# Three zero fills that run on fifteen DMA engines, without engine 2, in a decode step's forward and backward pass

## The chip, the cores and the metric

One core of a Trainium2 chip runs the whole program. The metric is the device time of one execution in microseconds (us); lower is better. Each kernel is run several times beside the kernel before, on the same chip, and all the runs that were compared here were in the fast state except one single run, of unknown state, which is marked. The kernel before takes 631.31 us (median of three runs, 631.11 to 631.31).

## The reference, cut to what matters

The reference is a transformer decode step of one token (attention over the last 4096 rows of a cache of 65,536, a gated MLP and modulated layer norms) together with its gradients. Two of its eleven outputs are the gradients of the two caches. Only the last 4096 of their 65,536 rows can be non-zero:

```python
W = min(4096, max(256, Sk // 4))                       # Sk = 65536, so W = 4096
k = jnp.repeat(k_cache[:, :, Sk - W:, :], rep, axis=1)
v = jnp.repeat(v_cache[:, :, Sk - W:, :], rep, axis=1)
...
_out, _vjp = jax.vjp(_f, A_x, A_k_cache, A_v_cache, ...)
return (_out0, *[jnp.asarray(_g) for _g in _grads])    # 2 x 4 heads x 61440 rows of zeros
```

So the kernel has to write 2 x 4 x 61,440 x 128 bf16 zeros, 120 MB (of 1024 KB each), besides loading the weights and storing their gradients.

## The kernel before

The zeros are written in 120 fills of 1 MB, issued by GpSimd wherever the schedule has room for them. Lists of counts (Z_FFN, Z_DWO and others) say how many follow each step.

```python
ZW = 4096
zeros = vt([P, ZW // 2], "zeros", FP8)            # 128 x 2 KB of zeros in SBUF
...
for og in (out_2, out_3):
    for g in range(G):
        region = og[0, g, 0:SKW, :].rearrange("r d -> (r d)").rearrange("(p x) -> p x", p=P)
        for i in range(region.shape[1] // ZW):
            zregions.append(region[:, i * ZW:(i + 1) * ZW])
zleft = list(zregions)
...
def zero(n, after=None):
    for _ in range(n):
        if len(zleft) <= keep[0]:
            return
        # per row: 2 KB of fp8 zeros in, a region of 8 KB seen as fp32 out
        ins = nc.gpsimd.dma_start(out=zleft.pop(0).bitcast(FP32), in_=zeros[:, :])
        if after is not None:
            dep(ins, after)
```

A fill has 128 rows of 8 KB. I take it as spread evenly over the 16 DMA engines of the page, 64 KB for each: at a sixteenth of the 429 GB/s that the program moves from 606 to 612 us, 64 KB takes 2.44 us, and successive fills near the end land 2.45 us apart. Most gradients are stored by GpSimd's DMAs as well; the rows of eight that Sync stores (`col_to_row_out`, in the trace eight packets of 256 bytes each) come up once below. The last DMA lands at 625.98 us, 3.5 us before the span ends.

## Time and profile before

| | before |
|---|---|
| median time | 631.31 us |
| span of the profiled run | 629.5 us |
| bytes moved by DMA | 256.42 MB, mean 407 GB/s |
| last landing, first of its 16 increments | 619.09 us |
| last landing, fifteenth increment | 620.75 us |
| last landing, sixteenth increment | 625.98 us |

From the page of the kernel before, the busy times of the compute engines, and the row of the DMA issues that belongs to the zero fills (count, size of one, median time from issue to landing):

```profile
PE 185.2 (29%) x3324; PEld 162.1 (26%) x3324; DVE 325.8 (52%) x728; ACT 212.8 (34%) x333; POOL 141.0 (22%) x224
...
out_dram<-zeros POOLq DMA_DIRECT2D x120, 1024.0 KB, 17.5
```

No compute engine is near its limit (52% at most), and a fill lands 17.5 us after its issue although one engine's share of it takes 2.45 us: about seven are in the queue (17.5 / 2.45). The remaining views of the kernel before are shown in the prediction.

Two ways of reading are used all through this text. A **landing** is the set of sixteen semaphore increments of one DMA; they stand in the trace with their times. I read them as one from each of the 16 DMA engines: between the fifteenth of the last landing (620.75 us) and its sixteenth (625.98) the program moves 20 to 26 GB/s, about a sixteenth of the 429 before. No record says which engine sent which. A **late** engine shows as a sixteenth increment far behind the fifteenth.

### The profile page before, as it was taken

To read this page: it belongs to the slowest core of one execution; us is meant where nothing else is said; L and a number is where in the kernel's file an instruction comes from. 1 tells how busy PE (TensorE), PEld (TensorE's weight loads), DVE (VectorE), ACT (ScalarE), POOL (GpSimd) and SP (SyncE) were. 2 spreads that over 40 slices of the span, in tenths; PEclk is the share of its full clock that TensorE was granted. 3 is DMA by queue.
4 is the path that set the end of the run, shared out by engine and by line. 5 is a ranking of instruction groups with operands and counts; after the bars stand their busy time and mean duration, and the time that the engine had idled before them with its cause. 6 is when DMAs were issued, how large, how long until landed. Compare 5 with 4: busy or idle time off the path is not lost.

```text
span 629.5 us, 8417 instructions
## 1 busy us (share of the span) xinstructions
PE 185.2 (29%) x3324; PEld 162.1 (26%) x3324; DVE 325.8 (52%) x728; ACT 212.8 (34%) x333; POOL 141.0 (22%) x224
## 2 busy tenths in 40 slices
PE   3877175632031211111111113304910022226100
PEld 3877155622021211111111112201700012225000
DVE  2442045204986784647565456999730089920400
ACT  2651156200035352424343233984700022225300
POOL 1001011103314232325312342222111013212320
PEclk9875588755555555555555555555755555555555
DMA  9999999999999999999999999999999999999994
GB/s 350 425 419 421 420 421 419 425 423 427 421 380 397 402 400 406 405 402 407 410 401 406 385 411 411 420 421 424 423 424 426 425 419 428 427 427 423 422 427 160
DMA packets 42183, 256.42 MB, mean 407 GB/s; under 512 B 4768, under 2 KB 4768, under 8 KB 17568
## 3 DMA queue, kind: packets, MB, share of 16 engines
q0 software_dynamic: 31104, 192.95, 80.2%
q1 hardware_dynamic: 10992, 62.93, 29.0%
q8 instruction: 26, 0.43, 0.3%
q14 instruction: 13, 0.11, 0.0%
q10 hardware_dynamic: 48, 0.01, 0.0%
HBM read 70.26 MB, written 185.60 MB: 406 GB/s over the span
## 4 chain that ended last, share of the span: by engine, by line
DMA 66%; DVE 13%; PE 6%; ACT 5%; issue 4%; POOL 3%; ACTq 0%; POOLq 0%; SPq 0%; DVEq 0%
DMA out_dram<-arena 35%; DMA arena<-in_B_w_gate_dram 8%; DMA arena<-in_A_wq_dram 7%; DVE arena L177 7%; DMA arena<-in_A_v_cache_dram 6%; DMA out_dram<-zeros 4%; DMA arena<-in_A_wo_dram 4%; ACT arena L791 1%; ACT arena L208 1%; DVE arena L181 1%; DVE fold_ps L181 1%; POOL out_dram L623 1%; PE tp_kv L407 1%; DMA rows<-in_c_dram 1%; POOL arena L506 1%
## 5 line engine op out<-in xcount | busy, mean ns | idle before, releaser
L142 POOL DMA_DIRECT2D out_dram<-zeros x120 | 65.5, 550 | 213.6 <-DMA out_dram<-zeros 58.5
L208 ACT ACTIVATE arena<-dug_b,h 128x512 bf16<-128x512 bf16 x112 | 71.4, 713 | 13.2 <-DVE dh2acc L177 12.1
L177 DVE CUSTOM_DVE_ANT_0 arena<-arena,dug_b 128x512 bf16<-128x512 bf16 x112 | 69.6, 684 | 0.4
L177 DVE CUSTOM_DVE_ANT_0 arena<-arena 128x1024 bf16<-128x1024 bf16 (+1 forms) x16 | 45.1, 2818 | 46.6 <-DMA arena<-in_w_mod_dram 39.2
L579 PE MATMUL gu_ps<-h_bf,arena 128*128 128x1 bf16 x448 | 16.0, 166 | 129.9 <-issue 97.8
L787 PEld LDWEIGHTS <-arena 8*128 8x128 bf16 x256 | 24.7, 127 | 105.8 <-issue 102.7
L579 PEld LDWEIGHTS <-arena 128*128 128x128 bf16 x448 | 14.1, 105 | 131.9 <-issue 98.3
L177 DVE CUSTOM_DVE_ANT_0 junk<-arena,b1k 128x1024 fp8e4<-128x1024 bf16 x28 | 34.2, 1223 | 15.1 <-DMA arena<-in_B_w_down_dram 14.6
L177 DVE CUSTOM_DVE_ANT_0 arena<-arena,b1k 128x1024 bf16<-128x1024 bf16 x32 | 37.2, 1219 | 0.0
L505 POOL DMA_DIRECT2D arena<-in_B_w_up_dram x14 | 12.7, 910 | 105.2 <-DMA out_dram<-arena 93.3
L791 ACT CAST arena<-ps_kv 128x512 bf16<-128x512 f32 x32 | 16.1, 696 | 59.7 <-DMA out_dram<-arena 59.7
L581 ACT ACTIVATE sg<-gu_ps 128x2 f32<-128x2 f32 x14 | 2.4, 171 | 94.8 <-PE gu_ps L579 94.8
L787 PE MATMUL ps_kv<-DO_hd,arena 8*128 8x128 bf16 x128 | 15.2, 277 | 60.5 <-ACT arena L791 59.7
L208 ACT ACTIVATE arena<-b1k,o_sh 128x1024 bf16<-128x1024 bf16 x24 | 27.2, 1152 | 11.0 <-DVE do_sh L177 11.0
L793 ACT ACTIVATE arena<-ps_kv 128x512 bf16<-128x512 f32 x32 | 16.1, 627 | 38.8 <-DMA out_dram<-arena 38.8
L169 DVE COPY arena<-tp_kv 128x1024 bf16<-128x1024 bf16 x19 | 13.0, 690 | 30.4 <-PE tp_kv L407 30.3
L407 PE MATMUL tp_kv<-ident_bf,arena 128*128 128x128 bf16 x256 | 21.8, 251 | 23.3 <-DMA arena<-in_A_k_cache_dram 13.7
L787 PE MATMUL ps_kv<-Q_hd,arena 8*128 8x128 bf16 x128 | 16.1, 296 | 38.9 <-ACT arena L793 38.9
L407 PEld LDWEIGHTS <-arena 128*128 128x128 bf16 x256 | 19.0, 114 | 26.1 <-DMA arena<-in_A_k_cache_dram 14.6
L410 ACT COPY arena<-tp_kv 128x1024 bf16<-128x1024 bf16 x13 | 13.2, 1012 | 34.9 <-PE tp_kv L407 34.9
L316 PEld LDWEIGHTS <-arena 128*128 128x128 bf16 x320 | 24.5, 119 | 0.0
L603 PE MATMUL bc_ps<-ident_bf,dug_bf 128*128 128x128 bf16 x56 | 14.5, 475 | 33.9 <-DVE hh L160 33.9
(224 smaller groups left out, 478.6 us busy)
## 6 DMA issues: line engine op xcount, KB each, us to landing
out_dram<-zeros POOLq DMA_DIRECT2D x120, 1024.0 KB, 17.5
out_dram<-arena POOLq DMA_DIRECT2D x32, 1024.0 KB, 19.5
out_dram<-arena POOLq DMA_DIRECT2D x36, 512.0 KB, 13.2
arena<-in_A_wq_dram SPq DMA_DIRECT2D x16, 1024.0 KB, 14.6
arena<-in_w_mod_dram SPq DMA_DIRECT2D x8, 1536.0 KB, 19.4
arena<-in_A_wo_dram SPq DMA_DIRECT2D x8, 1024.0 KB, 40.9
arena<-in_B_w_down_dram SPq DMA_DIRECT2D x14, 512.0 KB, 10.5
arena<-in_B_w_up_dram POOLq DMA_DIRECT2D x14, 512.0 KB, 11.3
```

The lines of the kernel that those rows point to most:

```text
L142: ins = nc.gpsimd.dma_start(out=zleft.pop(0).bitcast(FP32), in_=zeros[:, :])
L169: return nc.vector.tensor_copy(out=out, in_=a)
L177: return nc.vector.tensor_tensor_reduce(out=out, in0=w, in1=b, scale=1.0, scalar=0.0, op0=ALU.mult, op1=ALU.add, accum_out=acc)
L208: return nc.scalar.activation(out=out, in_=b, func=ACT.Copy, scale=col)
L316: nc.tensor.transpose(tp[:, nb * P:(nb + 1) * P], wm_t[j][:, c0:c0 + P], ident_bf[:, :])
L407: nc.tensor.transpose(tp[:, t8 * P:(t8 + 1) * P], src[:, g, t_ * DH:(t_ + 1) * DH], ident_bf[:, :])
L410: last = nc.scalar.copy(out=o, in_=tp[:, :])
L579: nc.tensor.matmul(gu[:, col + jj:col + jj + 1], lhsT=ug[:, k, j, jj::2], rhs=h2_bf[:, j:j + 1], start=(j == 0), stop=(j == KD - 1))
L603: nc.tensor.matmul(ps4[:, k // 2, :, k % 2], lhsT=r["dug_bf"][:, k:k + 1].broadcast_to([P, P]), rhs=ident_bf[:, :], start=(k == 0), stop=( ...
L787: nc.tensor.matmul(ps[:, t4 * DH:(t4 + 1) * DH], lhsT=rows[32 * g:32 * g + HG, t_ * P:(t_ + 1) * P], rhs=hd[32 * g:32 * g + HG, :], start= ...
L791: nc.scalar.copy(out=o, in_=ps[:, :])
L793: nc.scalar.activation(out=o, in_=ps[:, :], func=ACT.Copy, scale=float(scale))
```

## The change

Its intent: one DMA engine is about 5 us behind the others at the end (5.23 us in the last landing), so take three fills' worth of work (64 KB each) off that engine. The change takes it to be engine 2. Fills 78, 92 and 104 of the 120, counted from 0, write only 120 of their 128 rows, in a form meant for fifteen engines. No record names an engine or shows in which order DMAs take them. **Engine n** is therefore only a label in this text, for the engine that `SKIP = n` is meant to leave out, and "engines 0 to n" are those of the small DMA with n + 1 rows. The rows left out are written elsewhere, most of them by one early DMA of 180 KB. The core of the diff:

```diff
+SKIP = 2
+NARROW = (78, 92, 104)
...
+            region, narrow_ = zleft.pop(0)
+            first = None
+            if narrow_:
+                nc.gpsimd.inc_swdge_sem([], [], mode="reset_dge_cursor")
+                n = nlen - ncount.pop()
+                first = nc.gpsimd.dma_start(
+                    out=rest[0:2 * NS, n * 256:(n + 1) * 256].bitcast(FP32).rearrange("(t p) x -> p t x", t=2),
+                    in_=zeros[0:NS, 0:128].rearrange("p (t x) -> p t x", t=1).broadcast_to([NS, 2, 128]))
+                ins = nc.gpsimd.dma_start(
+                    out=region[8:P, :].bitcast(FP32).rearrange("(t p) x -> p t x", t=2),
+                    in_=zeros[0:60, :].rearrange("p (t x) -> p t x", t=1).broadcast_to([60, 2, ZW // 2]))
+            else:
+                ins = nc.gpsimd.dma_start(out=region.bitcast(FP32), in_=zeros[:, :])
...
     zero(Z_INIT)
+    nc.gpsimd.dma_start(out=rest[:, nlen * 256:].bitcast(FP32).rearrange("p (t x) -> t p x", t=16),
+                        in_=zeros[0:16, 0:nlen * 120].rearrange("t (p x) -> t p x", p=1).broadcast_to([16, 8, nlen * 120]))
+    if NS < 4:
+        nc.gpsimd.dma_start(out=rest[2 * NS:8, 0:nlen * 256].bitcast(FP32), in_=zeros[0:8 - 2 * NS, 0:nlen * 128])
```

`NS` is `SKIP + 1`, `nlen` is 3, and `rest` is the first 8 rows of the three changed fills' regions.

More of the change, by code (lines that the diff above doesn't have):

```diff
@@ L127 @@
                 zregions.append(region[:, i * ZW:(i + 1) * ZW])
-    zleft = list(zregions)
+    narrow = zregions[0:len(NARROW)]
+    wide = zregions[len(NARROW):]
+    zleft = []
+    while narrow or wide:
+        if narrow and (len(zleft) in NARROW or not wide):
+            zleft.append((narrow.pop(0), True))
+        else:
+            zleft.append((wide.pop(0), False))
+    nlen = len(NARROW)
+    ncount = list(range(1, nlen + 1))
+    NS = SKIP + 1
+    rest = out_2[0, 0, 0:SKW, :].rearrange("r d -> (r d)").rearrange("(p x) -> p x", p=P)[0:8, 0:nlen * ZW]
+    assert nlen * 2 <= 16
     keep = [sum(Z_END)]
@@ L141, in zero @@
                 return
-            ins = nc.gpsimd.dma_start(out=zleft.pop(0).bitcast(FP32), in_=zeros[:, :])
+            region, narrow_ = zleft.pop(0)
[9 more added lines that the diff above has]
+                    in_=zeros[0:60, :].rearrange("p (t x) -> p t x", t=1).broadcast_to([60, 2, ZW // 2]))
+            else:
+                ins = nc.gpsimd.dma_start(out=region.bitcast(FP32), in_=zeros[:, :])
             if after is not None:
-                dep(ins, after)
+                dep(first or ins, after)
     def new_ps(name="ps"):
@@ L844 @@
     col_to_row_out(dcv, out_9, "dc")
-    assert not zleft
+    assert not zleft and not narrow
 _INS = ['A_x', 'A_k_cache', 'A_v_cache', 'A_wq', 'A_wo', 'B_x', 'B_w_gate', 'B_w_up', 'B_w_down', 'c', 'w_mod', 'grad_out']
```

## The prediction

> **What bounds the kernel now.** I read the page first: the DMA rows of its 40 slices, the queues, the chain. Then I cut the end of the span into windows, then read the chain and the issues there, and last the semaphore increments that the trace records for every landing.
>
> The page: busy shares of the 16 DMA engines in slices of 15.7 us, their rate, and the queues.
>
> ```profile
> DMA  9999999999999999999999999999999999999994
> GB/s 350 425 419 421 420 421 419 425 423 427 421 380 397 402 400 406 405 402 407 410 401 406 385 411 411 420 421 424 423 424 426 425 419 428 427 427 423 422 427 160
> DMA packets 42183, 256.42 MB, mean 407 GB/s; under 512 B 4768, under 2 KB 4768, under 8 KB 17568
> ...
> q0 software_dynamic: 31104, 192.95, 80.2%
> q1 hardware_dynamic: 10992, 62.93, 29.0%
> ```
>
> The DMA engines are at 90% or more in every slice but the last, and from the 26th slice on they move 419 to 428 GB/s. No compute engine is over 52% busy on the same page. So the kernel is bound by the bytes on its DMA engines, and what can still be won late in the program is how evenly the sixteen finish. The last slice, with its 160, is where to look. The same end in windows (columns: stretch, length, five engines' busy time, clock, DMA share, GB/s):
>
> ```profile
> 606.00:612.00 6.00, 0.00 (x0) 0.00 (x0) 0.00 (x0) 0.00 (x0) 1.49 (x3) 0.50 1.09 429
> 612.00:617.00 5.00, 0.00 (x0) 0.00 (x0) 0.00 (x0) 0.00 (x0) 0.11 (x1) 0.50 1.15 431
> 617.00:619.00 2.00, 0.00 (x0) 0.00 (x0) 0.00 (x0) 0.00 (x0) 0.00 (x0) 0.50 1.06 393
> 619.00:620.75 1.75, 0.00 (x0) 0.00 (x0) 0.00 (x0) 0.00 (x0) 0.00 (x0) 0.50 0.37 131
> 620.75:622.00 1.25, 0.00 (x0) 0.00 (x0) 0.00 (x0) 0.00 (x0) 0.00 (x0) 0.50 0.07 26
> 622.00:624.00 2.00, 0.00 (x0) 0.00 (x0) 0.00 (x0) 0.00 (x0) 0.00 (x0) 0.50 0.07 25
> 624.00:626.00 2.00, 0.00 (x0) 0.00 (x0) 0.00 (x0) 0.00 (x0) 0.00 (x0) 0.50 0.06 20
> 626.00:629.50 3.50, 0.00 (x0) 0.00 (x0) 0.00 (x0) 0.00 (x0) 0.00 (x0) 0.50 0.00 0
> ```
>
> The reader is to see a step: all engines until 619, then for over five microseconds 25 to 26 GB/s at a DMA share of 0.07. That is one engine of sixteen (429 / 16 = 26.8 GB/s; 1/16 = 0.06), alone at its full rate. The chain that ended last agrees: it ends in zero fills and in their issues.
>
> ```profile
> 581.02 12.94 DMA out_dram<-zeros
> 593.96 0.28 issue
> 594.25 14.59 DMA out_dram<-zeros
> 608.83 0.28 issue
> 609.12 0.53 POOL out_dram L142
> ```
>
> The increments give the sizes. GpSimd's DMAs use eight semaphores in turn (432 increments each, 27 DMAs of 16), so each issue waits for the landing eight DMAs earlier: the fill issued at 609.12 waited for one that landed at 608.83. In the landing of the very last fill the first fifteen increments come from 619.09 to 620.75 and the sixteenth at **625.98**. In the ten landings before it the sixteenth is 5.2 to 5.3 us late too. Successive 1 MB fills are 2.45 us apart on every increment, so an engine does its 64 KB in 2.45 us, and the straggler is 5.23 / 2.45 = **2.1 fills behind**. It was 1.5 us behind at the fill landing at 390, 2.2 at 407, 3.3 at 453 and 4.05 at 541; around 476 it was 9 us behind and regained 5 of them by 490. After its last landing the span runs 3.5 us longer, and the measured time (631.31) is 1.8 us over the span (629.5).
>
> [...]
>
> **The change part by part.**
> (a) *Three fills leave engine 2 out.* By order of issue they are the zero fills numbered 78, 92 and 104 of 120, issued here at 387.5, 430.0 and 521.4 us and landing at 406.9, 453.0 and 541.3. Each writes 120 of 128 rows, 960 KB over fifteen engines, so 64 KB per engine as before. The fifteen lose nothing and gain nothing; engine 2 loses 3 x 2.45 = **7.35 us** of work. Its queue holds up to seven other DMAs at these times, some 17 us of work (the page's median from issue to landing of a fill is 17.5), so it goes on at once with the next DMA and the saving is not lost in idling.
> (b) *The left-out rows.* 3 x 8 rows x 8 KB = 192 KB are written elsewhere: one early DMA of 180 KB on all sixteen engines, one of 3 KB[...], and a 3 KB DMA ahead of each changed fill. The early one is 11.25 KB per engine, 11.25 / 64 x 2.45 = **0.43 us** on every engine. It is cut into 1440-byte pieces in place of 8 KB ones, and I allow 0.1 us for that. It falls while the engines are already full (350 GB/s in the first slice with its start-up, 425 in the second), so I count it whole, 0.53 us.
> (c) *GpSimd.* Five more issues at about 0.55 us (the page's mean for a fill) and three resets of the cursor[...]. GpSimd has 22% busy and waits for DMA landings in most of these places; the two early issues come before its next one at 12.87 us. All beside other work: 0. The three small DMAs each take one of the eight semaphores for a while, which leaves about seven large ones in flight; still 17 us.
> (d) *Sum.* Engine 2 ends at 625.98 - 7.35 + 0.53 = 619.2. The fifteen end at 620.75 + 0.53 = **621.3**, and now set the end. With the 3.5 us of tail and the 1.8 us between span and time: 621.3 + 3.5 + 1.8 = **626.6 us**, 4.7 us or 0.75% less. The choice in this is to take the fifteen's end as unmoved but for the 0.53 us. Two changed fills would put engine 2 at 625.98 - 4.90 + 0.53 = 621.6, nearly the same end; the third buys safety.
>
> **The rivals.**
> *The straggler is not engine 2,*[...]. Then engine 2 runs ahead idle and the straggler carries the extra 0.53 us: about 631.8 us. For it: no view names the engine. Against it: [...]a diff that picks one number was most likely found by measuring. I give it 8%.
> *The lag comes back.* The straggler's lag grew from 1.5 us at 390 to 5.2 at the end. If it is tied not to bytes but to waiting, for instance to the issues held back by its own late landings, then taking bytes away lets it fall behind again and the gain is only part: 628 to 629 us. Against it: the fills land 2.45 us apart on the sixteenth increment as on the others over the last 30 us, so it is a constant distance carried along by a full queue. 7%.
> *A new wait.* The reset or the small DMA ahead of a changed fill might make GpSimd wait until its queue is empty, three times some microseconds with the engines idle: 633 us or more. Nothing of it is in the profile; the 20 us of queued work would cover a short one. 4%.
> *More than the sum.* Issues of loads and stores in the chain wait for the straggler (landings at 486.5, 515.2, 536.1 and 556.0 come 4 us after the fifteenth increment). Without it they'd come 4 us earlier, and if the fifteen were starved there, time would be won too. But they run at 424 GB/s there, so at most about 0.5 us: 626.
>
> **Range and chances.** The sum is 626.6. Its two uncertain terms are the cost of (b), 0.3 to 1 us, and how close together the fifteen stay, about 0.5 us each way; the partial rival pulls the upper side out. So 625.6 to 628.4 for 8 in 10. A gain of over 2% would have to exceed 12.6 us, over twice all that the lag holds; a loss of that size needs the emptied queue. Faster 0.01, within 2% 0.98, slower 0.01.
>
> **What would show it.** Right: the 25 GB/s stretch at the end is gone or under 1 us, and the rate falls from over 390 to nothing within about 2.5 us; in the last landings the sixteenth increment follows the fifteenth within 0.5 us; the distance from the sixteenth to the fifteenth falls at each of the three fills; the last landing is near 621.3. Wrong: a stretch of 25 GB/s of five microseconds or more still stands there (another engine lags), landings with a lag that grows again after 541, the first fills landing over 1 us later than before (the early DMA costs more), or GpSimd idle for over 5 us just before a changed fill with the DMA rate dipping (a new wait).

What no trace or run shows is cut out of the prediction: its grounds for the number of the late engine and for the order of the engines, the engines of a 3 KB DMA, and an assumed duration of the resets. No term of its sum goes with them (the resets counted 0): it came to 620.75 + 0.53 + 3.5 + 1.8 = 626.6 us. Of the last eight increments of the 8-row output issued by Sync at 592.38, seven come from 597.15 to 598.39 and the eighth at 602.46. The 0.1 us for the finer pieces was an allowance when it was written; the trace of the changed kernel then showed its size. Eight of the 128 pieces of 1440 bytes, an engine's share, take 8 x 74 ns = 0.59 us, and the same 11.25 KB in packets of 8 KB at 348 ns (medians) would take 0.49.

## The result, and the profile after

The changed kernel takes **632.18 us** (median of 4 runs, 631.98 to 632.68) against 631.31 us (631.11 to 631.65, 4 runs beside it). The ratio is 1.0014, with a 95% interval of 0.9997 to 1.0032. Ratios in this text are the mean time of one kernel's runs over the mean of the other's runs of the same rounds, so not quite the ratio of the medians. By the interval the two can't be told apart, though all four runs lie above all four of before. The predicted 626.6 us with its range of 625.6 to 628.4 was wrong.

The page of the changed kernel, the same rows as in the prediction:

```profile
DMA  9999999999999999999999999999999999999994
GB/s 350 424 419 420 421 420 420 424 423 426 423 377 400 403 399 406 407 404 406 408 403 404 389 408 412 420 420 425 421 425 426 423 422 427 424 426 416 421 427 156
DMA packets 42503, 256.42 MB, mean 407 GB/s; under 512 B 4964, under 2 KB 5112, under 8 KB 17912
...
q0 software_dynamic: 31424, 192.95, 80.3%
q1 hardware_dynamic: 10992, 62.93, 28.7%
```

The bytes are the same, and the last slice nearly so (156 GB/s in place of 160). There are 320 packets more: 148 of the small DMAs and the finer cut left-out rows, less the 24 of 8 KB that these rows had, and 196 of 4 bytes. The end in windows (same columns as in the prediction):

```profile
612.00:617.00 5.00, 0.00 (x0) 0.00 (x0) 0.00 (x0) 0.00 (x0) 0.53 (x1) 0.50 1.13 425
617.00:619.00 2.00, 0.00 (x0) 0.00 (x0) 0.00 (x0) 0.00 (x0) 0.00 (x0) 0.50 1.18 438
619.00:620.75 1.75, 0.00 (x0) 0.00 (x0) 0.00 (x0) 0.00 (x0) 0.00 (x0) 0.50 0.56 201
620.75:622.00 1.25, 0.00 (x0) 0.00 (x0) 0.00 (x0) 0.00 (x0) 0.00 (x0) 0.50 0.07 26
622.00:624.00 2.00, 0.00 (x0) 0.00 (x0) 0.00 (x0) 0.00 (x0) 0.00 (x0) 0.50 0.08 29
624.00:626.00 2.00, 0.00 (x0) 0.00 (x0) 0.00 (x0) 0.00 (x0) 0.00 (x0) 0.50 0.07 25
626.00:628.00 2.00, 0.00 (x0) 0.00 (x0) 0.00 (x0) 0.00 (x0) 0.00 (x0) 0.50 0.00 0
```

The stretch at 25 to 29 GB/s is still there, now up to about 626.5: one engine is about as far behind as before (5.07 us in the last landing, 5.23 before). The last landing has its fifteenth increment at 621.43 us and its sixteenth at 626.50, where the kernel before had 620.75 and 625.98. The chain that ended last is the same too:

```profile
581.54 12.91 DMA out_dram<-zeros
594.46 0.28 issue
594.75 14.57 DMA out_dram<-zeros
609.32 0.28 issue
609.60 0.53 POOL out_dram L171
```

Each issue of it comes about 0.5 us later than in the kernel before (609.60 against 609.12), most likely the price of the left-out rows, and nothing gained for it.

Did the changed fills leave an engine out at all? They did. The small DMA in front of each of them has three pairs of packets of 512 bytes, which I read as one pair for each of its three engines, and no other DMA of the program has packets of that size (the trace has 18, three times six), so they can be found in the trace. They start at these times (the second packet of each pair, 10 ns later, is left out; the last two columns are that small DMA's fifteenth and sixteenth increments):

```
small DMA   engines 0, 1, 2, sorted by time    15th     16th
1           401.5   401.6   401.6              403.01   405.11
2           443.6   445.9   446.0              447.67   450.97
3           528.7   533.6   534.1              535.20   539.38
```

One of the three engines is 2.3 us ahead of the next at the second and 4.9 us ahead at the third: one fill after the first changed fill, two after the second. So the engine left out is one of the three that the small DMA uses; which of the three was not shown. But before any of this took effect, at the first small DMA, none of the three was late, while an engine somewhere was 2.1 us behind. **The late engine is not among 0, 1 and 2.** The relieved engine did not even keep its lead. In a DMA whose fifteenth increment comes at 569.5 us the first was 7.5 us ahead of it, in the last one 1.8 us. The lead shrank in the DMAs issued at 561.0, 571.0 and 581.0 us, each the first after GpSimd had issued nothing for 5.8 to 8.5 us. Behind the last two of these waits stands ScalarE, which waited 6.0 us for a DMA each time and went on at 566.67 and 576.70, 0.1 us after sixteenth increments (566.56 and 576.60), so after the late engine; the relieved engine has most likely emptied its queue there and stood idle.

### The profile page after: what moved, and what is told of

It reads as the page before. It is cut to its first block, busy times and chain, and to the rows that moved or that the text cites. A ratio compares the mean times of both kernels' runs of the same rounds, so it can differ in the third digit from the quotient of the medians.

```text
span 630.2 us, 8427 instructions
## 1 busy us (share of the span) xinstructions
PE 188.1 (30%) x3324; PEld 164.7 (26%) x3324; DVE 325.8 (52%) x728; ACT 212.9 (34%) x333; POOL 147.4 (23%) x229
## 4 chain that ended last, share of the span: by engine, by line
DMA 63%; DVE 14%; PE 10%; issue 4%; ACT 3%; POOL 3%; ACTq 0%; POOLq 0%; DVEq 0%; SPq 0%
DMA out_dram<-arena 29%; DMA out_dram<-zeros 9%; DMA arena<-in_B_w_gate_dram 8%; DVE arena L206 7%; DMA arena<-in_A_v_cache_dram 6%; DMA arena<-in_A_wo_dram 4%; DMA arena<-in_w_mod_dram 4%; DMA arena<-in_B_w_down_dram 2%; DVE arena L210 1%; DVE fold_ps L210 1%; PE tm_w L349 1%; PE tp_kv L440 1%; DMA rows<-in_c_dram 1%; DVE arena L202 1%; ACT arena L237 1%
## 5 line engine op out<-in xcount | busy, mean ns | idle before, releaser
L171 POOL DMA_DIRECT2D out_dram<-zeros x117 | 64.2, 551 | 201.2 <-DMA out_dram<-zeros 51.8
L612 PEld LDWEIGHTS <-arena 128*128 128x128 bf16 x448 | 14.1, 104 | 127.3 <-issue 95.1
L440 PE MATMUL tp_kv<-ident_bf,arena 128*128 128x128 bf16 x256 | 23.1, 260 | 22.5 <-DMA arena<-in_A_k_cache_dram 13.7
L440 PEld LDWEIGHTS <-arena 128*128 128x128 bf16 x256 | 20.1, 119 | 25.5 <-DMA arena<-in_A_k_cache_dram 14.6
L349 PEld LDWEIGHTS <-arena 128*128 128x128 bf16 x320 | 25.8, 123 | 0.0
```

What stands on the lines that cost most here:

```text
L171: ins = nc.gpsimd.dma_start(out=region.bitcast(FP32), in_=zeros[:, :])
L349: nc.tensor.transpose(tp[:, nb * P:(nb + 1) * P], wm_t[j][:, c0:c0 + P], ident_bf[:, :])
L440: nc.tensor.transpose(tp[:, t8 * P:(t8 + 1) * P], src[:, g, t_ * DH:(t_ + 1) * DH], ident_bf[:, :])
L612: nc.tensor.matmul(gu[:, col + jj:col + jj + 1], lhsT=ug[:, k, j, jj::2], rhs=h2_bf[:, j:j + 1], start=(j == 0), stop=(j == KD - 1))
```

## The experiments

What was to be told apart: which engine is late (theory A names engine 7; B one of 3 to 6), or whether the lag belongs to no engine's bytes at all (theory C, lag by waiting). All variants change `SKIP` and the shape of the small DMA, which is meant for `SKIP + 1` engines and cannot have 2 x 8 rows out of 8:

```diff
-SKIP = 2
+SKIP = 7            # or 5, 4, 3
...
-                    out=rest[0:2 * NS, n * 256:(n + 1) * 256].bitcast(FP32).rearrange("(t p) x -> p t x", t=2),
+                    out=rest[0:NS, n * 512:(n + 1) * 512].bitcast(FP32).rearrange("p (t x) -> p t x", t=2),
...
-    nc.gpsimd.dma_start(out=rest[:, nlen * 256:].bitcast(FP32).rearrange("p (t x) -> t p x", t=16),
-                        in_=zeros[0:16, 0:nlen * 120].rearrange("t (p x) -> t p x", p=1).broadcast_to([16, 8, nlen * 120]))
-    if NS < 4:
-        nc.gpsimd.dma_start(out=rest[2 * NS:8, 0:nlen * 256].bitcast(FP32), in_=zeros[0:8 - 2 * NS, 0:nlen * 128])
+    nc.gpsimd.dma_start(out=rest[:, nlen * 512:].bitcast(FP32).rearrange("p (t x) -> t p x", t=16),
+                        in_=zeros[0:16, 0:nlen * 112].rearrange("t (p x) -> t p x", p=1).broadcast_to([16, 8, nlen * 112]))
+    if NS < 8:
+        nc.gpsimd.dma_start(out=rest[NS:8, 0:nlen * 512].bitcast(FP32), in_=zeros[0:8 - NS, 0:nlen * 256])
```

The runs came in four groups, each on another chip. The kernel before took 631.29 to 631.52 us (medians) in all four. All results were correct.

### First group: engine 7, engine 5, and the change once more

Engine 7 left out:

> The changed kernel with engine 7 left out in place of 2 (the small DMA ahead of each changed fill runs on 8 engines[...]). Theory A, the straggler is engine 7: its last landing goes from 626.0 us to about 619, the fifteen set the end at about 621.3, no stretch at 25 GB/s is left, and the time is 626.6 us (626 to 627.5). Theory B, the straggler is one of engines 3 to 6: as in the changed kernel, last landing near 626.5, time 632 us, with engine 7 some 7 us ahead at the end. Theory C, the lag comes from waiting and not from one engine's bytes: the sixteenth increment stays about 5 us behind the fifteenth whichever engine is left out, 632 us.

Measured: 632.13 us, ratio 1.0008 (0.9993 to 1.0023), last landing 626.66. Theory A is out. The expected lead of 7 us at the end was not seen either, most likely for the reason given above: the relieved engine runs out of work. At the third small DMA one of the eight engines was 5.5 us ahead and another was late (table below).

Engine 5 left out (the edit with `SKIP = 5`):

> The same with engine 5 left out; the small DMA ahead of each changed fill has two 512-byte packets on each of engines 0 to 5. Theory A (engine 7 lags): no gain, about 632 us, and all twelve 512-byte packets of the third small DMA run by the time the fifteenth engine gets there, none 4 us later. Theory B: with the straggler among 3 to 5, two of the twelve packets run about 4 us after the rest; with engine 5 itself the straggler, 626.6 us. Theory C: 632 us.

Measured: 632.38 us, ratio 1.0012 (0.9992 to 1.0032), last landing 626.90, and one pair of the third small DMA 3.4 us behind the others. So the late engine is among 0 to 5.

Engine 7 left out of two fills (`NARROW = (78, 92)`):

> Engine 7 left out of two fills (numbers 78 and 92) in place of three. Theory A: the straggler does 2 x 2.45 us less and ends at 625.98 - 4.90 + about 0.4 (8 KB per engine of left-out rows in place of 11) = 621.5, within 0.3 us of the fifteen, so the time is 626.7 us, the same as with three. Theories B and C: about 632 us, as with three.

Measured: 631.85 us, ratio 1.0004 (0.9988 to 1.0021), last landing 626.46. With the wrong engine the count of fills gains nothing; what remains is the cost of the left-out rows, and this run sizes it: the last landing is 0.48 us later than in the kernel before with two fills and 0.68 with three, so a little over 0.2 us for each fill.

The changed kernel without any edit, on this chip:

> The changed kernel as it is, on this job's chip. If the straggler is the same engine on every chip (theory A or B): 632 us again, last landing 626.5, one engine 7 us ahead of the slow end of the fifteen. If which engine lags differs from chip to chip, and engine 2 lags on this one: 626.6 us, and then engine 7 left out gives 632 us.

Measured: 632.22 us, last landing 626.50, and again one of engines 0 to 2 ahead (528.1 against 532.4 and 533.3 us) and none late. The result is not one chip's. On this chip the late engine was thus 3, 4 or 5, and leaving out 5 had not helped.

### Second group: engines 4 and 3

So engines 4 and 3 were left.

> Engine 4 left out. So far: no late pair of 512-byte packets among engines 0 to 2 (changed kernel), one among 0 to 5 (engine 5 left out) and one among 0 to 7 (engine 7 left out), so the straggler is 3, 4 or 5, and leaving out 5 did not help. Theory A2, the lag belongs to one fixed engine's own work and that engine is 4: last landing about 621.3, 626.6 us. A3, it is engine 3: 632.2 us here, with one late pair among the ten packets of the third small DMA. Theory C, the lag comes from waiting and not from bytes: 632 us here and with engine 3 as well.

Measured: **627.14 us**, ratio 0.9936 (0.9919 to 0.9953). The last landing has its fifteenth and its sixteenth increment both at 621.51. The end of this kernel in windows:

```profile
617.00:619.00 2.00, 0.00 (x0) 0.00 (x0) 0.00 (x0) 0.00 (x0) 0.00 (x0) 0.50 1.08 401
619.00:620.75 1.75, 0.00 (x0) 0.00 (x0) 0.00 (x0) 0.00 (x0) 0.00 (x0) 0.50 0.54 197
620.75:622.00 1.25, 0.00 (x0) 0.00 (x0) 0.00 (x0) 0.00 (x0) 0.00 (x0) 0.50 0.05 13
622.00:624.00 2.00, 0.00 (x0) 0.00 (x0) 0.00 (x0) 0.00 (x0) 0.00 (x0) 0.50 0.00 0
```

The stretch at 25 GB/s is gone; from 620.75 on there are 13 GB/s for 1.25 us, then nothing. The gap from the fifteenth to the sixteenth increment fell from 2.07 to 0.12 us in the first changed fill, and from the third on it stayed under 0.1.

> Engine 3 left out; small DMA on engines 0 to 3. A2 (engine 4 lags): no late pair among the eight 512-byte packets of the third small DMA, 632.2 us. A3 (engine 3 lags): a pair that is late before the first changed fill and level with the others by the third, last landing about 621.3, 626.6 us. Theory C: a late pair in all three small DMAs and 632 us.

Measured: 632.38 us, ratio 1.0015 (1.0000 to 1.0030), last landing 626.61, and no late pair at any of the three small DMAs. The packets of all five kernels together, at the first small DMA (before anything was left out) and at the third (SKIP = 2 on the chip of the result, 5 and 7 on that of the first group, 3 and 4 on that of the second):

```
left out   small DMA on   first small DMA, start on each engine, sorted            16th
2          0 to 2         401.5 401.6 401.6                                        405.11
3          0 to 3         400.4 401.1 402.2 402.6                                  405.19
4          0 to 4         400.4 401.0 401.7 402.4 404.2                            405.19
5          0 to 5         400.2 400.8 401.7 401.8 403.0 404.4                      405.43
7          0 to 7         400.7 401.1 401.5 401.8 402.0 402.2 402.3 404.3          405.21

left out   small DMA on   third small DMA                                          16th
2          0 to 2         528.7 533.6 534.1                                        539.38
3          0 to 3         530.0 532.5 533.8 534.6                                  539.48
4          0 to 4         533.1 533.1 533.8 534.0 535.1                            535.74
5          0 to 5         528.9 532.9 533.3 533.8 535.6 539.0                      539.73
7          0 to 7         527.7 533.2 533.6 534.3 534.3 534.5 534.5 538.8          539.51
```

At the first small DMA a start at 404.2 to 404.4, about 1 us before the sixteenth increment, appears as soon as engine 4 is among the engines, and never without it; on the second group's chip that is 0 to 4 against 0 to 3. **The late engine is 4**, the one that `SKIP = 4` leaves out. This takes the small DMAs of four to eight rows to use the first four to eight engines of one order; no trace shows that order, but all five kernels fit it. The end times agree: of the three kernels whose small DMA reaches engine 4, only the one that leaves out 4 has no late pair at the third, and its sixteenth increment comes at 535.74 in place of 539.5 or later. An early one (527.7 to 530.0) is there in every kernel that relieved a wrong engine.

### Third group: once more, and the number of fills

> Engine 4 left out of three fills, once more, in a job of its own. If engine 4 lags on every chip that these jobs get, as the runs so far would have it: 627.1 us, last landing 621.5. If which engine lags is the chip's own: on another chip 632 us.

Measured: 627.07 us, ratio 0.9930 (0.9915 to 0.9945), last landing 621.15, on a third chip. So the late engine was 4 on the two chips where it could be told, and 3 or 4 on that of the first group. This version is the fastest, and beats both kernels.

Engine 4 left out of two fills (`SKIP = 4`, `NARROW = (78, 92)`):

> Engine 4 left out of two fills (78 and 92). The sum says that engine 4 then ends at 625.98 - 4.90 + 0.4 = 621.5, level with the fifteen: 627.1 us, within 0.3 of three fills, with an increment gap of 0.3 us or less at the end. If the lag returns in proportion to what is taken away, the gap would be 1 to 2 us and the time 628 to 629.

Measured: 627.60 us, ratio 0.9940 (0.9926 to 0.9955); fifteenth 621.33, sixteenth 621.87. The sum was 0.4 us short, so the third fill seems worth about 0.5 us and not nothing: all four runs lie above the four with three fills, though the intervals of the two ratios overlap.

Engine 4 left out of one fill (`SKIP = 4`, `NARROW = (92,)`):

> Engine 4 left out of one fill (92). The sum says that engine 4 ends at 625.98 - 2.45 + 0.2 = 623.7, about 2.6 us behind the fifteenth, so 629.2 us: half the gain. If the lag is not a matter of bytes, no such step of 2.45 us.

Measured: 629.70 us, ratio 0.9971 (0.9954 to 0.9988); fifteenth 621.53, sixteenth 623.98. The windows of its end:

```profile
619.00:620.75 1.75, 0.00 (x0) 0.00 (x0) 0.00 (x0) 0.00 (x0) 0.00 (x0) 0.50 0.65 239
620.75:622.00 1.25, 0.00 (x0) 0.00 (x0) 0.00 (x0) 0.00 (x0) 0.00 (x0) 0.50 0.10 33
622.00:624.00 2.00, 0.00 (x0) 0.00 (x0) 0.00 (x0) 0.00 (x0) 0.00 (x0) 0.50 0.05 16
624.00:626.00 2.00, 0.00 (x0) 0.00 (x0) 0.00 (x0) 0.00 (x0) 0.00 (x0) 0.50 0.00 0
```

The lone engine's stretch is shorter by one fill's time. The steps of the sixteenth increment are thus 626.5 (no fill taken off it, left-out rows paid), 624.0, 621.9, and then 621.5 or 621.2, where the fifteen others set the end. The first step is 2.5 us and the second 2.1, but the first starts from a kernel that pays for three fills' left-out rows. Like for like, two fills taken off engine 4 in place of engine 7 bring the sixteenth from 626.46 to 621.87, 4.59 us, against 4.90 in the sum. The lag shrinks with the bytes taken off one engine, and theory C is out. Nor does the lag come back because it was cut: in the kernel before, the gap from the fifteenth to the sixteenth increment grew by 1.15 us from 541 to 589 us, and with one fill taken off, where the gap is less than half as large, by 1.2 us over the same stretch (1.19 to 2.40).

### Third and fourth group: what engine 4 does besides

Why engine 4? In the kernel before the gap from the fifteenth to the sixteenth increment grew from 3.9 us (landing at 538.7) to 5.2 (landing at 589.0), a stretch with 380 tensor engine instructions by the windows view (191 matmuls and 189 weight loads). From there to the end there are two, and the gap stayed between 5.2 and 5.4. So I added tensor engine instructions where there are none, to the kernel before:

```diff
+    spare = new_acc("spare")
+    for i in range(512):             # 256 in the second
+        nc.tensor.matmul(spare[:, i % 64:i % 64 + 1], lhsT=dmod_b2[:, (i % 16) * P:(i % 16 + 1) * P],
+                         rhs=cs_bf[:, 0:1], start=True, stop=True)
     assert not zleft
```

The 16 KB packets of the expectation come from the page of the kernel before: 26 packets, 0.43 MB, on queue 8, which it calls "instruction", for 6648 tensor engine instructions, so 256 for each packet (an estimate; the page does not say whose instructions these are).

> The kernel before with 512 more matmuls of one column at the end of the tensor engine's program, into a spare bank: 1024 more instructions, so four more 16 KB packets on queue 8 if that queue fetches them. They do no other harm (the tensor engine is idle there). If those packets are engine 4's extra work, its lag at the end goes from 5.2 to about 7.6 us and the time from 631.4 to about 633.8. If they ride on another engine, the sixteenth increment stays at 626.0, and another increment falls back by about 2.4 us behind the rest.

Measured, in a single run of unknown state: 634.26 us, last landing 628.40, so **2.42 us later** than before. Its end in windows, and its added matmuls in the timeline (start, length, engine, line, what, count, and in brackets the idle time before):

```profile
620.75:622.00 1.25, 0.00 (x0) 0.00 (x0) 0.00 (x0) 0.00 (x0) 0.00 (x0) 0.50 0.20 72
622.00:624.00 2.00, 0.00 (x0) 0.00 (x0) 0.00 (x0) 0.00 (x0) 0.00 (x0) 0.50 0.08 29
624.00:626.00 2.00, 0.00 (x0) 0.00 (x0) 0.00 (x0) 0.00 (x0) 0.00 (x0) 0.50 0.07 25
626.00:628.00 2.00, 0.00 (x0) 0.00 (x0) 0.00 (x0) 0.00 (x0) 0.00 (x0) 0.50 0.07 25
```

```profile
591.83 6.00 PE L847 MATMUL spare<-cs_bf,arena 128*128 128x1 bf16 x218
600.61 3.57 PE L847 MATMUL spare<-cs_bf,arena 128*128 128x1 bf16 x128 [2.79 <-issue]
607.63 3.57 PE L847 MATMUL spare<-cs_bf,arena 128*128 128x1 bf16 x128 [3.45 <-issue]
613.01 1.17 PE L847 MATMUL spare<-cs_bf,arena 128*128 128x1 bf16 x38 [1.80 <-issue]
```

Between the runs of added matmuls the tensor engine stands idle for 2.79, 3.45 and 1.80 us, the last two after 128 matmuls, 256 instructions with their weight loads; the profile names no cause. One engine alone now runs on to 628.40 (at 25 to 29 GB/s from 622), and the fifteenth increment, too, is later than before (622.19 against 620.75). The size is the expected one, but the packets that I had named do not fit in time. The four added 16 KB packets on queue 8 start at 598.3, 605.3, 610.8 and 617.2 us. The sixteenth increment was already 0.33 us later than in the kernel before at 594.3 and 0.86 later at 597.3, ahead of the first of them; it was 2.44 later at 615.0, ahead of the last, and 2.42 later at the end. The delay grows while the added matmuls run, not when those packets do.

> The kernel before with 256 added matmuls at its end in place of 512, so 512 added instructions. The 1024 of the run before moved the last landing by 2.4 us (628.4 against 626.0), 2.4 ns each. If the straggler pays per tensor engine instruction, half of it: last landing 627.2, 632.6 us. If it pays once for something else that the added block does, as much as before, 628.4.

Measured: 633.09 us, ratio 1.0029 (1.0000 to 1.0058), last landing 627.23, so 1.25 us later for 512 instructions, half of 2.42 for 1024.

The same 256 matmuls with 64 columns in place of one (`rhs=ident_bf[:, 0:64]`, output `spare[:, 0:64]`):

> The same 512 added instructions, but each matmul has 64 columns in place of 1 and so works longer. If the straggler pays per instruction: 627.2 again, 632.6 us. If it pays for the tensor engine's work, reads or power, clearly more than with one column.

Measured: 632.86 us, ratio 1.0025 (0.9996 to 1.0055), last landing 627.02, 1.04 us later for 512 instructions. This run was already 0.17 us ahead of the kernel before when the added matmuls began, so what it lost while they ran is the same again. The increments of the three runs, as us later than in the kernel before (whose trace is from another chip), in three landings, named by the time of the sixteenth increment in the kernel before:

```
            landing 591.5   landing 601.4   last landing (626.0)
            16th            16th            16th    15th    14th
pe_fetch    +0.01           +1.29           +2.42   +1.44   +1.31
pe_half     +0.04           +1.23           +1.25   +1.30   +1.17
pe_wide     -0.17           +1.01           +1.04   +1.15   +1.02
```

From the first to the last of these landings the late engine lost 2.41, 1.21 and 1.21 us for 1024, 512 and 512 instructions: 2.4 ns for each, whether a matmul has one column or 64. With 256 added matmuls, which had run by 602 us, the delay was complete in the second landing. That the late engine is 4 in these runs as well is taken from the other groups; none of these runs left it out.

The 16 KB packets show themselves elsewhere. In `pe_half` they start at 598.2 and 605.4. The fifteenth increment's delay jumps from 0.14 to 1.65 us between 597.4 and 600.2 us, the fourteenth's from 0.15 to 1.28 between 606.1 and 608.5, and the sixteenth's stays at 1.22 to 1.26 from 602.6 on; `pe_wide` shows the same. So each packet most likely set back one of the other fifteen engines by some 1.2 us, and the packets are not the late engine's extra work. What that work is was not shown: the packets in the trace do not tell, and no run was made to find it. Every run on record comes with a span and a granted clock, so whether the lag is there when nothing is recorded stays open too. Nor do the instructions explain all of the growth: 380 x 2.4 ns is 0.9 us of the 1.3 us between 538.7 and 589.0. The times of these three runs are 2.8, 1.8 and 1.6 us over those of before, 0.4 to 0.6 us more than the last landings moved.

## Why the prediction was wrong

The step that failed is in part (a), taken over from the change's own name: "*Three fills leave engine 2 out* ... engine 2 loses 3 x 2.45 = 7.35 us of work", with engine 2 put equal to the straggler in the sum "Engine 2 ends at 625.98 - 7.35 + 0.53 = 619.2". The work was taken off one of engines 0 to 2, as the early pairs show, but the late engine is 4. The first rival, "*The straggler is not engine 2*", is what happened. It had 8% and named 631.8 us; measured were 632.18.

Point by point:

- *The bound.* Right. The kernel is bound by its DMA engines and ends with one of them alone for 5.2 us. (The prediction reads its last stretch as 25 to 26 GB/s; the third of the three windows has 20.)
- *The evidence for engine 2.* Too weak for what I built on it. Nothing in the trace favoured 2, as the text itself says ("no view names the engine"); no trace shows which engines an eight-row output uses. I let "a diff that picks one number was most likely found by measuring" carry the rest. To put 92% on trust in the change's choice was the mistake.
- *The order of the engines.* Not shown by any record. The leads of 2.3 and 4.9 us on one of engines 0 to 2, and the success with `SKIP = 4` alone (627.14 us, against 632.13 to 632.38 with 2, 3, 5 and 7), agree with the order that the change counts on.
- *"The saving is not lost in idling."* It held for engine 4 in the experiments, and did not for engine 2: its lead of 7.5 us had shrunk to under 2 by the end. Only the late engine could use the relief.
- *(b), the left-out rows.* Right: 0.53 us forecast, 0.52 measured on the sixteenth increment (625.98 to 626.50) and 0.68 on the fifteenth. The match to 0.01 is luck: the sixteenth moved by 0.68 with engine 7 left out of three fills, and the runs do not split the cost into its parts.
- *(c), GpSimd.* Right in what it said of the end: neither a reset nor a small DMA made the queue run dry (405 to 426 GB/s in the changed kernel from 390 to 450 us and from 515 to 545), and with the right engine the whole sum came out within 0.5 us.
- *The sum for the right engine.* 621.3 for the fifteen and 626.6 us in all, against 621.5 and 621.2 and 627.1 us measured. "Nearly the same end" with two fills was off by 0.5 us.
- *"The lag comes back"* and *"a new wait"*: shown wrong by the runs with engine 4. *"More than the sum"*: wrong as well. With engine 4 relieved, the issue of the second to last fill comes at 604.59 us in place of 609.12, and yet the fifteen land where they did in the changed kernel (621.43 and 621.51).

## What to carry to other kernels

Late in a program that is bound by DMA, the distance of the last engine from the other fifteen in the final landings is what evening out can win (here it was 5.23 us, and 4.35 to 4.38 were won against the runs beside), and it can be read in time and in bytes before anything is changed. Which engine that is must be measured and not taken over from elsewhere: a small DMA with a packet size of its own on engines 0 to n showed a late packet here as soon as n reached the late engine (from n = 4 on a start at 404.2 to 404.4 us, with n = 2 and 3 none after 402.6), and the two kernels with n = 3 and 4, on one chip, settled it. Each added tensor engine instruction set the late engine back by 2.4 ns here, so fewer and larger matmuls may help even where the tensor engine is idle most of the time; this last point is an inference from the three runs that added instructions, none here took any away, and it may hold for recorded runs alone.
